# Attention, gated product and a second layer in one kernel: three weight conversions of the first batch moved behind its last group, two filling products fewer, and the second batch's groups four steps later

## The chip, the cores and the metric

The kernel runs on one core of a Trainium2 chip. The metric is the device time of one execution in microseconds; the median of several executions counts. A profiled execution gives a trace, whose engines are named PE (TensorE, matrix products), PEld (its weight loads), ACT (ScalarE), DVE (VectorE) and SP (SyncE, which here issues every DMA on one queue).

## The reference, cut to what matters

```python
# q, k, v: 4 batches, 8 heads, 576 positions, 64 wide
scores = (q @ k.T) / 8          # heads 0-3: the last 32 positions
                                # heads 4-7: 32 positions, every 4th
attn = softmax(where(mask, scores, -1e9))
x = (attn @ v)                  # 2304 tokens x 512
a = x @ w_a; b = x @ w_b        # 512 x 1536 each
y = (a * b) @ w_out             # 1536 x 512
h = y @ w_in                    # 512 x 2048
g = max(h, 0) + alpha * min(h, 0)
out = g @ w_out2                # 2048 x 512
```

The weights arrive as 64-bit floats and are turned into 32-bit floats on the chip.

## The kernel before, in words

**Tiles and steps.** The 2304 tokens are four token tiles of 512, 512, 512 and 768 (TILES). The program is written as a row of numbered steps. `step(products)` runs what was hung on that step before the products (`before`), the products, what was hung behind them (`after`), one round of the running jobs (`convey`), and last the loads in `behind`. Steps 0 to 16 are the first batch's attention. Step 17 begins token tile 0: for each of 12 blocks f of 128 columns of w_a and w_b there are three steps, twelve products into bank pa (x times w_a), twelve into pb (x times w_b), and then `flush`, twelve products of the block before with w_out into four banks accA. In every twelve there are four chunks c, each of three products: high by high, high by low, low by high part (lines L518, L519, L520), since each 32-bit number is held as the sum of two shorter ones.

**Attention.** A batch has 12 groups of three query blocks. Group i passes in the first batch through: scores on PE in step i (sp, L377); `largest` on DVE (L392), which is interleaved with `weights` of the group before (L413, L415, L417); `exps` on ACT, three of them (L406); transposition on PE in step i + 2 (tp, L429), its copy by ACT (`moved`, L434); the product with v in step i + 3 (ap, L442), and `placed`, a copy into the high part of x by ACT (L471) and the low part by DVE (L478, L476). Chunk c of x is complete with group 3c + 2, so chunk 3 only with group 11, placed in step 14. The second batch's groups go in pairs beside token tile 0: `visit_scores` (banks sa) at the steps in `slots`, `visit_turn` three steps later. Token tile 1 takes their result.

**Conversions.** Number n of the weight conversions is a job in `queue`: n = 0 and 1 are w_a and w_b of block 0, 2 and 3 those of block 1, 4 is w_out of block 0, and so on, three for a block. It begins with its load, `lead` steps ahead of step k. From step k on it issues two ACT operations (L189, which scales the high words; L192, the low words), a DVE operation that joins them (L195), an ACT copy to the high part (L224) and a DVE subtraction for the low part (L227). The tuple `apart` spreads them over further steps. The joined 32-bit block is also stored to DRAM two steps later (wad, wof; L202), and a buffer of five has to wait for that store. Loads are L207; the loads of a group are L341 (q, k) and L346 (v), those of v into five places, so that v of group i waits for the product of group i - 5.

**Filling products.** `heat(n)` multiplies a tile of zeros into bank pb, which nobody reads then (L611). ZEROS gives their number for steps 0 to 11; there are also five ahead of step 0. `begin` starts block 0's pa and pb with the chunks of x that exist, in steps 12 to 14.

**Order.** Up to the end of step 22 `in_source_order` keeps PE, ACT and DVE in the order in which the code issues. Behind that a scheduler at compile time places the instructions on each engine by its own estimate. Every engine then runs its row in order. SP's row also holds stores, which wait for DVE, so a load can stand behind a store.

Of the kernel before, what the change touches and what calls it, by code (L numbers as in the profile page):

```python
# [24 lines left out]
NC = DM // 128  # L25
# [7 lines left out]
NG = NST // GS  # L33
# [2 lines left out]
TILES = [(0, 512), (512, 512), (1024, 512), (1536, 768)]  # L36
N_PLAIN = 3
ONCE = 4, 12
ZEROS_FIRST, ZEROS = 5, (3, 0) + 10 * (1,)

HT = 384
NP = NT // (2 * HT)
# [22 lines left out]
def tile_kernel(ctx: ExitStack, tc: tile.TileContext, qk, v, mask, wab, wo1, w2, alpha, out):  # L65
# [38 lines left out]
    xh, xl = cut(rt, 0, 4, 512), cut(rt, 2048, 4, 512)  # L104
# [39 lines left out]
    n_start = NC * NG + 5  # L144
    n_tiles = len(TILES)
    start_of = [n_start + 3 * NFA * t + t for t in range(n_tiles)]
# [3 lines left out]
    before, after, now = {}, {}, [0]  # L150

    def at_step(table, k, fn):
        table.setdefault(k, []).append(fn)

    def step(products=None):
        k = now[0]
        for fn in before.pop(k, []):
            fn()
        if products:
            products()  # L160
        for fn in after.pop(k, []):
            fn()
        if k not in held:
            convey()
        while behind:
            behind.pop(0)()
        now[0] += 1


    queue, belt, behind = [], [], []  # L170

    def convey():

        for job in belt[::-1 if now[0] < start_of[1] else 1]:
            if next(job, "end") == "end":
                belt.remove(job)
        while queue and queue[0][0] <= now[0]:
            job = queue.pop(0)[1]
            next(job)
            belt.append(job)  # L180
# [102 lines left out]
    ws, wo = {}, {}  # L283
# [54 lines left out]
    def load_qk(n):  # L338
        if n < B * NC * NG:
            tqs[n] = t = (qk_ring if n >= NC * NG else qk_first).next()  # L340
            in_order(n, nc.sync.dma_start(out=t, in_=qk[n // (NC * NG), n % (NC * NG)]))  # L341

    def load_v(n):
        if n < B * NC * NG:
            tvs[n] = t = (v_ring if n >= NC * NG else v_first).next()[:KT].rearrange("p (s j d) -> p s j d", j=2, d=D)
            in_order(n, nc.sync.dma_start(out=t, in_=v[n // (NC * NG), n % (NC * NG)]))  # L346
# [175 lines left out]
    def contract(acc, wh, wl, xh, xl, n, cs=range(NC)):  # L522
        for c in cs:
            mm3(acc[:, :n], wh[:, c * 128:(c + 1) * 128], wl[:, c * 128:(c + 1) * 128],
                xh[:, c, :n], xl[:, c, :n], c == 0, c == NC - 1)
# [13 lines left out]
    def bank(tag):  # L539
        return ps.tile([128, 512], F32, tag=tag, name=tag)  # L540
# [26 lines left out]
    xn[1] = cut(ft, 2048, 4, 512)  # L567

    for i in range(4, NC * NG + 3):
        at_step(after, max(0, i - 4) if i < NC * NG else i - 1, lambda i=i: behind.append(lambda: load_qk(i)))  # L570
    for i in range(1, NC * NG + 3):
        at_step(after, i - 1 if i < 3 else i if i < NC * NG else i + 5, lambda i=i: behind.append(lambda: load_v(i)))
    at_step(after, 1, lambda: behind.append(lambda: nc.sync.dma_start(out=mk[:, 2:], in_=mask[:, 2:])))
    first = [Group(0, i) for i in range(NC * NG)]
    stages = [(after, "moved", 2), (after, "placed", 3), (before, "scores", 0), (before, "transposed", 2)]
# [12 lines left out]
    due += [(3 * f + 5, 3 * f - 2, "o", f, 0) for f in range(NFA)]  # L588
    n, k = 0, 0
    while due:  # L590
        k = (7, 9, 11)[n] if n < 3 else max(k + 1, 13)
        lead = 2 if n < 2 else min(n + 2, 6) if n < ONCE[1] else 2
        apart = (1, 0, 1, 1) if n < 2 else (1, 0, 0, 1) if n < 3 else (0, 0, 0, 1 if k < n_start else 0)
        job = min((x for x in due if n_start + x[1] <= k), default=None)
        if job:
            due.remove(job)
            places = raw_once if ONCE[0] <= n < ONCE[1] else raw_ring
            if job[2] == "a":
                job_w(k - lead, lead, places, apart, *job[3:])
            else:  # L600
                job_o(k - lead, lead, places, apart, job[3])
            n += 1
# [18 lines left out]

    begun = []

    def begin(j, *cs):

        if not begun:
            begun.extend((bank("pa"), bank("pb")))
        contract(begun[j], ws[0][:, 2 * j], ws[0][:, 2 * j + 1], xh, xl, 512, cs)

    begins = len(nc.cur_bb.bb.instructions)  # L630
    heat(ZEROS_FIRST)
    for k in range(n_start):
        if k < 12:
            step(lambda: heat(ZEROS[k]))
        elif k < 15:
            step(lambda: [begin(*x) for x in (((0, 0),), ((0, 1),), ((0, 2), (1, 0, 1, 2)))[k - 12]])
        else:
            step()
    at_step(after, start_of[1], lambda: tc.keep_in_program_order(nc.sync.dma_start(out=al, in_=alpha)))
# [85 lines left out]
        for f in range(NFA):  # L725
            reload_o(start_of[t] + 3 * f, t, f)
    for t in range(3):
        slots = [start_of[t] + (3 if t == 0 else 0) + int(j * (2.5, 2.64, 2.3)[t]) for j in range(NC * NG)]
        groups = [Group(t + 1, i) for i in range(NC * NG)]
        pairs = [groups[j:j + 2] for j in range(0, NC * NG, 2)]  # L730
        for j in range(len(pairs) + 1):
            k = slots[2 * j] if j < len(pairs) else slots[-1] + 2
            visit_scores(k, pairs[j] if j < len(pairs) else [], pairs[j - 1] if j else [])
            if j < len(pairs):
                visit_turn(k + 3, pairs[j])
# [4 lines left out]
    for n, job in enumerate(jobs[JOBS_A:JOBS_P]):  # L740
        at, lead = JOBS_AT[n]
# [62 lines left out]
    k = start_of[N_PLAIN - 1]  # L804
# [24 lines left out]
    for t, (t0, n) in enumerate(TILES[:N_PLAIN]):  # L829
        assert now[0] == start_of[t], (now[0], start_of[t])  # L830
        if t < 2:
            xn[t + 2] = xn_pair if t else cut(ft, 0, 4, 512)
        for f in range(NFA):
            final = f == NFA - 1
            if f == 0:
                accs = None
            wf = ws[f]
            early = (t, f) == (0, 1)
            started = (t, f) == (0, 0)
            cs = [NC - 1] if started else range(NC)  # L840
            pa = begun[0] if started else bank("acc2" if early else "pa")
            g = g_tile(n)
            box = []
            at_step(after, now[0] + 1, lambda g=g, pa=pa: nc.scalar.copy(g, pa[:, :n]))
            step(lambda: contract(pa, wf[:, 0], wf[:, 1], xh, xl, n, cs))
            pb = begun[1] if started else bank("acc3" if early else "pb")
            k = now[0]
            at_step(after, k + 1, lambda g=g, pb=pb: nc.vector.tensor_tensor(out=g, in0=g, in1=pb[:, :n], op=ALU.mult))
            at_step(after, k + 1 if final else k + 2, lambda g=g, box=box: split_g(box, g, n))
            step(lambda: contract(pb, wf[:, 2], wf[:, 3], xh, xl, n, cs))  # L850
            if final and t + 1 < N_PLAIN:
                for c in range(NC):
                    at_step(after, now[0], lambda c=c: split_x(xh, xl, xn[t + 1], c, TILES[t + 1][1]))
            if f == 1:
                accs = new_accs(f"A{t}")
                prev = (accs, *prev[1:])
            step(flush if f else None)
            prev = (accs, wo_of(t, f), box, n, f, NFA, x1d, t)
            if (t, f) == (0, 1):
                in_source_order(begins)  # L860
        step(flush)
# [106 lines left out]
    for f in range(NFA):  # L968
# [4 lines left out]
        ws = factors.pop(f)  # L973
# [280 lines left out]
```

## Time and profile before

| what | value |
|---|---|
| runs | 878.32, 876.09 and 878.98 us, median 878.32 us |
| the profiled execution | 876.4 us, of which 874.6 us are its span |
| busy share of the span | PE 98%, PEld 89%, DVE 72%, ACT 61% |
| instructions | 15640 |

The profiled execution is 1.9 us under the median of the runs shown. Busy shares are means over the whole span; what a change in one place is worth is read from that place.

### The profile page before, as it was taken

The numbers are of one execution on the slowest core, as the hardware profiler recorded it, in microseconds if no ns is written. First come the engines' busy times: TensorE is split into PE (matmuls) and PEld (weight loads), VectorE is DVE, ScalarE is ACT, GpSimd is POOL, SyncE is SP. The second block draws the span as 40 slices with busy tenths as digits, with TensorE's granted clock in tenths as the row PEclk, the third lists the DMA queues.
The fourth block names the chain that finished last, engine by engine and source line by source line (L and its number), as shares of the span: only waits on it lengthen the run. The fifth ranks groups of instructions, "written<-read, shape, count | busy, mean of one in ns | idle before, by whom it ended". The sixth has DMA issues, their size and how long they took to land.

```text
span 874.6 us, 15640 instructions
## 1 busy us (share of the span) xinstructions
PE 861.2 (98%) x5418; PEld 781.5 (89%) x5418; DVE 628.0 (72%) x1450; ACT 537.5 (61%) x1195; POOL 0.7 (0%) x6
## 2 busy tenths in 40 slices
PE   8898999999999999999999999999999999999998
PEld 5677888888888887889999999999999999999998
DVE  5768773646767678869797837898565896567954
ACT  7889873555666567655554637775565855565542
POOL 0000000000000000000000000000000000000000
PEclk9799999999999999999999999999999999999999
DMA  9969961589799888999565559878888887778875
GB/s 278 348 203 350 352 210 61 172 283 334 253 322 330 290 294 284 324 314 316 192 229 170 192 213 303 260 240 262 275 243 245 256 268 224 230 247 258 272 223 184
DMA packets 108125, 225.28 MB, mean 258 GB/s; under 512 B 12304, under 2 KB 27408, under 8 KB 108048
## 3 DMA queue, kind: packets, MB, share of 16 engines
q1 hardware_dynamic: 108048, 224.30, 78.6%
q8 instruction: 43, 0.70, 0.3%
q14 instruction: 34, 0.28, 0.1%
HBM read 169.72 MB, written 54.53 MB: 256 GB/s over the span
## 4 chain that ended last, share of the span: by engine, by line
PE 89%; DMA 6%; DVE 3%; ACT 1%; issue 1%; SPq 1%; ACTq 0%; DVEq 0%
PE acc L1163 20%; PE at L869 12%; PE pb L869 8%; PE pa L869 8%; PE accA L518 4%; PE accA L519 4%; PE accA L520 4%; PE pa L518 4%; PE pa L519 4%; PE pa L520 4%; PE pb L518 4%; PE pb L519 3%; PE pb L520 3%; DMA wsd<-rt 3%; PE tp L429 2%; PE sa L442 2%
## 5 line engine op out<-in xcount | busy, mean ns | idle before, releaser
L1163 PE MATMUL acc<-rt 128*128 128x384 f32 x1008 | 187.6, 334 | 0.0
L1163 PEld LDWEIGHTS acc<-rt 128*128 128x128 f32 x1008 | 175.8, 188 | 0.4 <-ACT ft L1146 0.4
L278 ACT CAST rt<-ft 128x512 fp32r<-128x512 f32 (+3 forms) x165 | 103.6, 636 | 89.1 <-DMA wsd<-rt 22.8
L281 DVE TENSOR_TENSOR rt<-ft,rt 128x512 fp32r<-128x512 f32 (+3 forms) x165 | 115.8, 708 | 58.8 <-ACT rt L278 57.7
L869 PE MATMUL at<-rt 128*128 128x384 f32 x414 | 84.3, 335 | 0.0
L885 ACT COPY ft<-at 128x384 f32<-128x384 f32 x105 | 49.9, 475 | 51.6 <-PE at L869 51.0
L869 PEld LDWEIGHTS at<-rt 128*128 128x128 f32 x414 | 72.7, 188 | 0.5 <-ACT ft L885 0.4
L518 PE MATMUL accA<-rt 128*128 128x512 f32 (+1 forms) x160 | 62.5, 392 | 2.3 <-ACT rt L278 2.3
L519 PE MATMUL accA<-rt 128*128 128x512 f32 (+1 forms) x160 | 61.9, 387 | 0.2 <-DVE rt L281 0.2
L520 PE MATMUL accA<-rt 128*128 128x512 f32 (+1 forms) x160 | 61.2, 384 | 0.0
L406 ACT ACTIVATE ft<-ft 128x96 f32<-128x96 f32 x144 | 52.2, 367 | 12.6 <-DVE ft L392 12.6
L195 DVE SCALAR_TENSOR_TENSOR ft<-ft 128x512 uint32<-128x512 uint32 x60 | 41.2, 687 | 22.8 <-ACT ft L192 16.9
L281 DVE TENSOR_TENSOR rt<-gx,rt 128x768 fp32r<-128x768 f32 x43 | 41.1, 957 | 22.3 <-ACT rt L278 22.0
L869 PE MATMUL pb<-rt 128*128 128x384 f32 x276 | 56.0, 337 | 0.1
L869 PE MATMUL pa<-rt 128*128 128x384 f32 x276 | 55.2, 334 | 0.0
L869 PEld LDWEIGHTS pb<-rt 128*128 128x128 f32 x276 | 48.1, 188 | 1.8 <-DVE gx L882 0.9
L192 ACT ACTIVATE ft<-ft 128x512 uint32<-128x512 uint32 x60 | 40.4, 673 | 14.2 <-DMA ft<-in_w 14.1
L278 ACT CAST rt<-gx 128x768 fp32r<-128x768 f32 x43 | 36.0, 836 | 21.1 <-PE acc L1163 16.9
L869 PEld LDWEIGHTS pa<-rt 128*128 128x128 f32 x276 | 48.5, 188 | 0.0
L869 PE MATMUL at<-rt,rx 128*128 128x384 f32 x216 | 44.0, 337 | 1.5 <-ACT ft L885 1.5
L189 ACT ACTIVATE ft<-ft 128x512 f32<-128x512 f32 x60 | 40.1, 670 | 6.6 <-DMA ft<-in_w 5.7
L869 PEld LDWEIGHTS at<-rt,rx 128*128 128x128 f32 x216 | 37.7, 188 | 2.7 <-ACT ft L885 2.5
(157 smaller groups left out, 1763.5 us busy)
## 6 DMA issues: line engine op xcount, KB each, us to landing
rt<-wsd SPq DMA_DIRECT2D x318, 256.0 KB, 3.2
wsd<-rt SPq DMA_DIRECT2D x112, 256.0 KB, 5.0
ft<-in_w SPq DMA_DIRECT2D x32, 512.0 KB, 5.6
ft<-in_qk SPq DMA_DIRECT2D x48, 208.0 KB, 5.4
ft<-in_wab SPq DMA_DIRECT2D x19, 512.0 KB, 5.5
rt<-wod SPq DMA_DIRECT2D x19, 512.0 KB, 5.1
rx<-wod SPq DMA_DIRECT2D x17, 512.0 KB, 4.7
ft<-in_v SPq DMA_DIRECT2D x48, 144.0 KB, 5.7
```

The costliest lines, as they stand in the source:

```text
L189: held(nc.scalar.activation(f, high.bitcast(F32), AF.Prelu, scale=2.0 ** -112, alpha=-2.0 ** 32))
L192: nc.scalar.activation(low, low, AF.Copy, scale=0.933 * 2.0 ** -29)
L195: nc.vector.scalar_tensor_tensor(out=fi, in0=fi, scalar=3, in1=low, op0=ALU.logical_shift_left, op1=ALU.bitwise_or)
L278: hi_eng.copy(hi, x)
L281: lo_eng.tensor_tensor(out=lo, in0=x, in1=hi.bitcast(F32), op=ALU.subtract)
L406: nc.scalar.activation(self.et[:, s], self.st[:, s], AF.Exp, bias=self.sm[:, 0, s:s + 1], scale=-1.0, accum_out=self.sm[:, 1, s:s + 1])
L518: nc.tensor.matmul(acc, lhsT=wh, rhs=rh, start=first, stop=False)
L519: nc.tensor.matmul(acc, lhsT=wh, rhs=rl, start=False, stop=False)
L520: nc.tensor.matmul(acc, lhsT=wl, rhs=rh, start=False, stop=last)
L869: nc.tensor.matmul(acc[:, :HT], lhsT=a, rhs=x[:, b, c], start=start and c == k == 0, stop=c == 1 and k == 2, skip_group_check=not start,)
L885: nc.scalar.copy(out, acc[:, :HT])
L1163: nc.tensor.matmul(acc[a][:, :HT], lhsT=u, rhs=q[:, b, i % 2], start=new and first and k == 0, stop=last and k == 2, skip_group_check=not new,
```

## The change: what it does

Conversions 1, 2 and 3 begin at steps 10, 15 and 16 (they began at 9, 11 and 13), and the ACT copy of conversion 1 now stands behind the last group's `placed`. Conversions from 4 on go at step 18 and after, one in each step (14 and after). Their loads move with them. The filling products of steps 5 and 6 go (one each). Block 0's pb is not begun early: all its twelve products stand in step 18, and pa's chunks 0 and 1 are in step 12, chunk 2 in step 14. The second batch's first visit goes from step 20 to step 24 and the visits follow each other a little more closely; the last goes from step 49 to step 50. Its first three loads of q and k move four steps later, those of v one.

```diff
-ZEROS_FIRST, ZEROS = 5, (3, 0) + 10 * (1,)
+ZEROS_FIRST, ZEROS = 5, (3, 0, 1, 1, 1, 0, 0, 1, 1, 1, 1, 1)
+HEAD = (7, (1, 0, 1, 1)), (10, (1, 0, 2, 0)), (15, (0, 0, 0, 0)), (16, (1, 0, 0, 0))
...
-        at_step(after, max(0, i - 4) if i < NC * NG else i - 1, lambda i=i: behind.append(lambda: load_qk(i)))
+        at_step(after, max(0, i - 4) if i < NC * NG else i + 3, lambda i=i: behind.append(lambda: load_qk(i)))
...
-        k = (7, 9, 11)[n] if n < 3 else max(k + 1, 13)
-        lead = 2 if n < 2 else min(n + 2, 6) if n < ONCE[1] else 2
-        apart = (1, 0, 1, 1) if n < 2 else (1, 0, 0, 1) if n < 3 else (0, 0, 0, 1 if k < n_start else 0)
+        k, apart = HEAD[n] if n < 4 else (max(k + 1, 18), (0, 0, 0, 1 if k < n_start + 4 else 0))
+        lead = (2, 3, 4, 4)[n] if n < 4 else 5 if n < ONCE[1] else 2
...
-            step(lambda: [begin(*x) for x in (((0, 0),), ((0, 1),), ((0, 2), (1, 0, 1, 2)))[k - 12]])
+            step(lambda: [begin(c) for c in ((0, 1), (), (2,))[k - 12]])
...
-        slots = [start_of[t] + (3 if t == 0 else 0) + int(j * (2.5, 2.64, 2.3)[t]) for j in range(NC * NG)]
+        slots = [start_of[t] + (7 if t == 0 else 0) + int(j * (2.25, 2.64, 2.3)[t]) for j in range(NC * NG)]
...
-            pb = begun[1] if started else bank("acc3" if early else "pb")
+            pb = bank("acc3" if early else "pb")
...
-            step(lambda: contract(pb, wf[:, 2], wf[:, 3], xh, xl, n, cs))
+            step(lambda: contract(pb, wf[:, 2], wf[:, 3], xh, xl, n))
```

The lines of the changed kernel are one higher than those named above, up to some 640.

ACT's row from the exps of group 11 on, before; L189 and L192 are first operations of conversions, L224 their copies, tp and ap with a number the groups:

```order
L406 ACTIVATE ft<-ft 128x96 x3
L189 ACTIVATE ft<-ft 128x512
L434 COPY ft<-tp_10_474 96x384
L471 CAST rt<-ap_9_478 128x128
L471 CAST rt<-ap_9_478 128x48
L192 ACTIVATE ft<-ft 128x512
L224 CAST rt<-ft 128x512
L434 COPY ft<-tp_11_503 96x384
L471 CAST rt<-ap_10_507 128x80
L471 CAST rt<-ap_10_507 128x96
L189 ACTIVATE ft<-ft 128x512
L192 ACTIVATE ft<-ft 128x512
```

and the same place now:

```order
L407 ACTIVATE ft<-ft 128x96 x3
L193 ACTIVATE ft<-ft 128x512
L435 COPY ft<-tp_10_464 96x384
L472 CAST rt<-ap_9_468 128x128
L472 CAST rt<-ap_9_468 128x48
L435 COPY ft<-tp_11_493 96x384
L472 CAST rt<-ap_10_497 128x80
L472 CAST rt<-ap_10_497 128x96
L472 CAST rt<-ap_11_512 128x32
L472 CAST rt<-ap_11_512 128x128
L225 CAST rt<-ft 128x512
L190 ACTIVATE ft<-ft 128x512
```

Of the conversions only the second operation of conversion 1 is left between the exps of group 11 and its `placed`; the copy of conversion 1 and the whole of conversions 2 and 3 stand behind it.

SP's row from the load of v for group 6 (in_v) to that of group 9 and one row on, before; in_wab and in_wo are loads of weights:

```order
L346 DMA ft<-in_v 96x384
L207 DMA ft<-in_wab 128x512 x2
L341 DMA ft<-in_qk 128x416
L346 DMA ft<-in_v 96x384
L207 DMA ft<-in_wab 128x512
L207 DMA rf<-in_wab 128x512
L346 DMA ft<-in_v 96x384
L207 DMA rf<-in_wo 128x512
L346 DMA ft<-in_v 96x384
L207 DMA rf<-in_wab 128x512
```

and now, from the same load of v on:

```order
L347 DMA ft<-in_v 96x384
L208 DMA ft<-in_wab 128x512
L342 DMA ft<-in_qk 128x416
L347 DMA ft<-in_v 96x384 x4
L208 DMA ft<-in_wab 128x512
L347 DMA ft<-in_v 96x384
L208 DMA ft<-in_wab 128x512
L203 DMA wad<-ft 128x512
L208 DMA rf<-in_wo 128x512
L208 DMA rf<-in_wab 128x512 x2
```

From there to the load of v for group 9 there were five weight loads and now there is one; the store of conversion 0 now stands ahead of the weight loads from number 4 on.

PE's row where block 2's pb and the first flush stand, before; accA_0 to accA_3 are the flush's banks, pa here is already block 3's:

```order
L518 MATMUL pa<-rt 128x512
L518 MATMUL pb<-rt 128x512
L519 MATMUL pb<-rt 128x512
L520 MATMUL pb<-rt 128x512
L518 MATMUL pb<-rt 128x512
L519 MATMUL pb<-rt 128x512
L520 MATMUL pb<-rt 128x512
L518 MATMUL pb<-rt 128x512
L519 MATMUL pb<-rt 128x512
L518 MATMUL accA_0_671<-rt 128x512
```

and the place of the first flush now, straight behind block 1's pb (acc_600):

```order
L521 MATMUL acc_600<-rt 128x512
L519 MATMUL accA_0_619<-rt 128x512
L520 MATMUL accA_0_619<-rt 128x512
L378 MATMUL sa_0_665<-ft 64x96 x2
L378 MATMUL sa_1_666<-ft 64x96 x2
L378 MATMUL sa_0_665<-ft 64x96 x2
L378 MATMUL sa_1_666<-ft 64x96 x2
L521 MATMUL accA_0_619<-rt 128x512
L519 MATMUL accA_1_620<-rt 128x512
```

Before, the scheduler had put the first product of block 3's pa ahead of block 2's pb and the first flush into the middle of that pb; now the flush of block 0 begins ahead of block 2. From token tile 1 on PE's row is the same in both kernels.

## Rows read from the trace of the kernel before

**Rows 1.** The page, its first line.

```profile
span 874.6 us, 15640 instructions
```

**Rows 2.** Waits of PE over the span: us in total, times, longest.

```profile
PE at L869 <- ACT ft L885: 1.5, 2, 0.8
```

**Rows 3.** Windows: length; busy PE, PEld, DVE, ACT, POOL (instructions); granted clock; DMA share; GB/s.

```profile
5.00:10.00 5.00, 3.85 (x57) 2.61 (x55) 2.73 (x25) 3.85 (x20) 0.00 (x0) 1.00 1.04 294
...
25.00:30.00 5.00, 2.69 (x34) 1.88 (x32) 3.53 (x19) 4.73 (x20) 0.00 (x0) 0.82 1.03 327
30.00:35.00 5.00, 5.00 (x29) 3.31 (x29) 2.72 (x12) 3.63 (x11) 0.00 (x0) 0.50 1.05 359
35.00:40.00 5.00, 5.00 (x25) 4.00 (x23) 4.34 (x11) 4.53 (x10) 0.00 (x0) 0.66 1.04 398
...
65.00:70.00 5.00, 2.69 (x12) 1.93 (x11) 4.66 (x23) 5.00 (x18) 0.00 (x0) 1.00 1.00 335
```

**Rows 4.** Timeline of PE: start, us, instruction, [idle before <- releaser].

```profile
15.92 0.39 PE L611 MATMUL pb<-zeros 128*128 128x512 bf16 x1
16.24 0.71 PE L377 MATMUL sp<-ft 64*64 64x96 f32 x12
...
27.16 0.57 PE L442 MATMUL ap<-ft 96*64 96x64 f32 x12 [1.43 <-ACT rt L224]
...
29.14 0.91 PE L442 MATMUL ap<-ft 96*64 96x64 f32 x12 [0.69 <-DMA ft<-in_v]
...
41.14 0.73 PE L377 MATMUL sa<-ft 64*64 64x96 f32 x24
...
44.66 0.39 PE L518 MATMUL acc<-rt 128*128 128x512 f32 x1
...
47.38 0.39 PE L518 MATMUL pa<-rt 128*128 128x512 f32 x1
```

**Rows 5.** Chain of work that ended last, first 45 us: start, us, what.

```profile
19.75 9.26 DMA ft<-in_v
```

**Rows 6.** Timeline of ACT, first batch.

```profile
17.45 0.47 ACT L434 COPY ft<-tp 96x384 f32<-96x384 f32 x1
...
18.17 0.38 ACT L406 ACTIVATE ft<-ft 128x96 f32<-128x96 f32 x1
...
19.26 0.66 ACT L189 ACTIVATE ft<-ft 128x512 f32<-128x512 f32 x1
...
25.94 0.69 ACT L192 ACTIVATE ft<-ft 128x512 uint32<-128x512 uint32 x1
26.48 0.65 ACT L224 CAST rt<-ft 128x512 fp32r<-128x512 f32 x1
...
27.77 0.49 ACT L471 CAST rt<-ap 128x32 fp32r<-128x32 f32 x2 [0.27 <-PE ap L442]
28.02 0.37 ACT L406 ACTIVATE ft<-ft 128x96 f32<-128x96 f32 x1
...
35.58 0.48 ACT L471 CAST rt<-ap 128x32 fp32r<-128x32 f32 x2
```

**Rows 7.** Timeline of DVE, weights of group 11.

```profile
30.06 0.16 DVE L413 TENSOR_SCALAR ft<-ft 128x3 f32<-128x3 f32 x1
...
30.47 0.46 DVE L417 TENSOR_TENSOR ft<-ft 128x288 f32<-128x288 f32 x1
```

**Rows 8.** Timeline of DVE, low part of conversion 11.

```profile
63.27 0.69 DVE L227 TENSOR_TENSOR rt<-ft,rt 128x512 fp32r<-128x512 f32 x1 [1.16 <-ACT rt L224]
```

**Rows 9.** Timeline of PE, blocks 2 and 3.

```profile
50.93 0.50 PE L518 MATMUL pa<-rt 128*128 128x512 f32 x1 [0.68 <-ACT ft L844]
...
69.72 0.97 PE L518 MATMUL accA<-rt 128*128 128x512 f32 x3 [2.31 <-ACT rt L278]
```

**Rows 10.** DMA from 65 to 110 us: packets, bytes, rate.

```profile
DMA packets 6453, 15.65 MB, mean 348 GB/s; under 512 B 736, under 2 KB 2080, under 8 KB 6450
```

**Rows 11.** DMA from 43 to 65 us.

```profile
DMA packets 1820, 4.31 MB, mean 196 GB/s; under 512 B 205, under 2 KB 496, under 8 KB 1816
```

More of the change, by code (lines that the diff above doesn't have):

```diff
@@ L569, in tile_kernel @@
     for i in range(4, NC * NG + 3):
-        at_step(after, max(0, i - 4) if i < NC * NG else i - 1, lambda i=i: behind.append(lambda: load_qk(i)))
+        at_step(after, max(0, i - 4) if i < NC * NG else i + 3, lambda i=i: behind.append(lambda: load_qk(i)))
     for i in range(1, NC * NG + 3):
-        at_step(after, i - 1 if i < 3 else i if i < NC * NG else i + 5, lambda i=i: behind.append(lambda: load_v(i)))
+        at_step(after, i - 1 if i < 3 else i if i < NC * NG else i + 6, lambda i=i: behind.append(lambda: load_v(i)))
     at_step(after, 1, lambda: behind.append(lambda: nc.sync.dma_start(out=mk[:, 2:], in_=mask[:, 2:])))
@@ L622, in tile_kernel, with begin @@
     begun = []
-    def begin(j, *cs):
+    def begin(c):
         if not begun:
-            begun.extend((bank("pa"), bank("pb")))
-        contract(begun[j], ws[0][:, 2 * j], ws[0][:, 2 * j + 1], xh, xl, 512, cs)
+            begun.append(bank("pa"))
+        contract(begun[0], ws[0][:, 0], ws[0][:, 1], xh, xl, 512, [c])
     begins = len(nc.cur_bb.bb.instructions)
```

## The prediction

> **What bounds the kernel now.** I read the waits of PE first. What it waits for lies almost wholly in the first 75 us: after that only one pair of waits of 1.5 us in all is over half a microsecond [rows 2]. So a microsecond that PE gains early is kept to the end, and the question is only what the first 75 us lose. I then read windows of 5 us. From 25 to 30 us PE is busy 2.69 of 5 us, and from 28 us on the clock granted to TensorE is halved (1.2 instead of 2.4 GHz): shares 0.82, 0.50 and 0.66 in three windows [rows 3]. At full speed these would have held 5 x (0.18 + 0.50 + 0.34) = 5.1 us more of PE's time. Then I read PE's timeline for what came before the fall: a wait of 1.43 us at 27.16 and one of 0.69 us at 29.14, both ahead of a product with v [rows 4]. The chain of waits names the cause: the load of v for group 9, issued at 19.75 us, took 9.26 us to land [rows 5], with DMA's share at 1.03 in that stretch [rows 3]; five weight loads stand between the loads of v for groups 6 and 9 on SP. The wait at 27.16 is put down to ACT: with an ACT copy for a conversion, 26.48, just ahead of it, the in-order row of ACT is the other half of the trouble [rows 6]. Last, PE's later timeline has two more waits, 0.68 us at 50.93 and 2.31 us at 69.72 [rows 9].
>
> **The change, part by part.**
> *First batch, ACT.* From the exps of group 7 (18.17) to those of group 11 (28.02) ACT runs nearly without a gap [rows 6]. In that piece two conversions' ACT operations stand; now one of them, the second operation of conversion 1, goes behind the exps of group 11: 26.48 - 25.94 = 0.54 us. The 0.27 us wait at 27.77 was for a product delayed by the loads and goes too [rows 6]. A filling product costs PE 16.24 - 15.92 = 0.32 us [rows 4]; two go, but ACT was nearly full beside them, so they bring between 0 and 0.64 us. I take 0.3. Exps of group 11 then start at 28.02 - 0.54 - 0.27 - 0.3 = 26.9.
> *From there to block 1.* With durations as an upper estimate: exps 1.09 (19.26 - 18.17) to 28.0; second operation of conversion 1 0.54 to 28.5; copy of group 10 0.47 to 29.0; `placed` of group 9 0.49 to 29.5 [rows 6]. DVE's weights of group 11 take 30.47 + 0.46 - 30.06 = 0.87 [rows 7], to 28.9, and the transposition fits in by 29.5. Copy of group 11 0.47 to 30.0; its product with v 0.57 at the full clock [rows 4] to 30.5; `placed` 0.49 to 31.0; copy of conversion 1 0.65 to 31.7 [rows 6]; DVE's low part 0.69 [rows 8] to 32.4. Block 0's pb, all twelve products, takes 47.38 - 44.66 = 2.72 us [rows 4]; two of the first three need no low part, so it ends at about 35.0. Block 1 can begin there. Before, the second batch's scores at 41.14 stood in that place and are now later: 41.1 - 35.0 = **6.1 us**. Not beginning pb early costs what PE idles around 31 us, which is in this sum. This supposes that TensorE's clock stays up. The two ends: if it is low for as long as before, the 5.1 us above go and 1.0 us is left; if ACT's operations overlap as their starts in the rows do, about 1 us more, 7.1 us.
> *Loads of v.* Group 9's v is now behind one weight load instead of five. Its place comes free with group 4's product, near 17 us; even at 9.26 us again it would land at 26.5, when that product is due.
> *Conversions 2 and 3.* Six ACT operations behind `placed` of group 11. Conversion 2 needs 0.66 + 0.69 + 0.65 on ACT [rows 6] and two DVE operations of 0.69 [rows 8]: ready near 35, when block 1's pa starts and its first two products need only the high part. Conversion 3 has until block 1's pb, 2.72 us later. No cost taken; up to 1 us if the chain is later than worked out.
> *Block 3's early product and the flush of block 2.* The wait of 0.68 us is that of a product of block 3's pa for the copy of block 2's pa, which stood right ahead of it in PE's row; a flush stands between them now. The wait of 2.31 us is that of block 2's flush for a split which ACT reached late, with the second batch's exps ahead of it; those come four steps later, and ACT's row at that time is emptier by them. Both go: 0.68 + 2.31 = **3.0 us** [rows 9].
> *Conversions from 4 on, four steps later.* The work is the same. From a conversion's end to the step that needs it there were seven steps and are three, some 9.5 us. DMA has to move 0.79 MB for a conversion (128 x 1024 words of four bytes in, half as many out) and in the mean 0.16 MB for the visits (two groups' 352 KB in 4.5 steps) in each step; a step is 2.72 us and a share of a visit, about 3.2 us, so 297 GB/s are wanted where 348 were moved from 65 to 110 us [rows 10]. It is hidden if the three steps hold. The store of conversion 0 that now stands ahead of weight loads waits for DVE until about 23 us, when nothing behind it is due before 33.
> *New waits* that the fixed rows of ACT and SP may bring cannot be read off: between 0 and the 2.31 us of the worst one shown [rows 9]; I take 0.5, as the work per step is under what each engine can do.
> *Sum*, against the profiled execution: 876.4 - 6.1 - 3.0 + 0.5 = 867.8 (its span is 874.6 us [rows 1], and 1.8 us around it stay). That execution lies 1.9 us below the median of the runs shown (878.32), so the median forecast is **869.7**.
>
> A rule speaks against it. The row first: in the window from 5 to 10 us PE is busy only 3.85 of 5 us and the clock stays at 1.00, but from 25 to 30 us with 2.69 of 5 it falls [rows 3]. The Trainium skill, page "TensorE: Matmul & The Clock Gate", section "A second HAM failure mode: psum-queue depth-cycling", says that many short idle spells of PE between groups of products can make the clock drop again and again. Steps 5 and 6, without a filling product and paced by ACT, are such spells; by that rule the clock would fall there already, by the row it does not. What that would cost stands under the first rival.
>
> **The rivals.**
> *The clock falls again in the first batch*, in the two steps without filling products or in the spells near 26 and 31 us. For it: the waits of 1.43 and 0.69 us were enough before [rows 4]. Against it: now I find under 1 us of idle in such a stretch instead of these 2.1, and from 65 to 70 us PE is busy as little as from 25 to 30 with the clock at 1.00 [rows 3]. If it is low for as long as before, the 5.1 us come back: 867.8 + 5.1 + 1.9 = 874.8.
> *The gain is partly given back at the weights.* Block 4's pa now comes, by 35.0 + 9 x 2.72 (three pairs, three flushes) + 2.7 for the visits, at 62.2, while the low part of conversion 11, which it needs, ended at 63.27 + 0.69 = 64.0 before [rows 8]. Were it no earlier, PE would wait 1.8 us: 871.5. Against it: ACT idles less and has fewer exps ahead.
> *Slower: the three steps do not hold.* From 43 to 65 us DMA moved only 196 GB/s [rows 11], since SP stood at stores. 4.31 MB in 22 us are 4.5 steps' need where PE passes 7; one such stretch makes the weights 2.5 steps late, which three steps of reserve cover. It decides from a reserve overrun by 2.7 steps (8.6 us), so from a bit over two such stretches. With three, 7.5 - 3 = 4.5 steps x 3.2 = 14.4 us: 867.8 + 14.4 + 1.9 = 884. Against it: from 65 us on DMA kept 348.
> *Nothing moves*: the loads of v are late anyway and the chain of ACT sets the same end: 878. Against it stands the one load instead of five.
>
> **How the numbers follow.** Chances: forecast 0.60 (its own range 867.5 to 871.2, from 7.1 instead of 6.1 us to 2.3 us of new waits, less rounding), clock 0.15, weights given back 0.15, slower 0.07, nothing 0.03. The predicted time is 869.7. The range reaches to the clock's case, which leaves out the last two and the very best: 866.5 to 875.2. About 0.3% (2.6 us) is what a measurement of this kernel can tell from no change; by the cases, faster 0.90, within it 0.03, slower 0.07.
>
> **What would show it.** Right: granted clock 1.00 in all windows from 20 to 45 us; exps of group 11 near 27; block 1's pa (bank acc2) near 35; no wait of PE over 1 us between 35 and 75; the second batch's first scores only after the start of block 0's flush. Wrong: a share under 1.00 near 17 or 28 us; PE waiting in token tile 0 for low parts of conversions (L228 or L225 as releaser); loads of v again 9 us under way.

## The result and the profile after

| | before | after |
|---|---|---|
| median of 4 runs | 878.15 us (876.09 to 878.98) | 867.32 us (866.77 to 868.62) |
| profiled execution | 876.4 us, span 874.6 us | 867.85 us, span 866.1 us |

The ratio is 0.9882, with a 95% interval of 0.9861 to 0.9903: 10.8 us less. Between the two profiled executions it is 8.55 us.

I read the windows of 5 us first (length; busy PE, PEld, DVE, ACT, POOL with their instructions; granted clock; DMA share; GB/s):

```profile
20.00:25.00 5.00, 4.40 (x68) 3.19 (x68) 4.05 (x25) 5.00 (x25) 0.00 (x0) 1.00 0.75 230
25.00:30.00 5.00, 4.00 (x39) 2.85 (x40) 4.05 (x24) 4.57 (x19) 0.00 (x0) 1.00 0.96 348
30.00:35.00 5.00, 4.86 (x41) 3.58 (x40) 3.57 (x13) 4.38 (x11) 0.00 (x0) 1.00 0.89 297
35.00:40.00 5.00, 5.00 (x24) 4.14 (x23) 2.99 (x5) 4.17 (x9) 0.00 (x0) 1.00 0.98 322
```

PE is busy 4.00 us from 25 to 30 us, where it was 2.69, and the granted clock stays at 1.00 where it was 0.82, 0.50 and 0.66 [rows 3]. ACT's timeline has the exps of group 11 at 27.08 us and one conversion operation (28.15) between them and the three `placed` copies of groups 9, 10 and 11:

```profile
27.08 0.39 ACT L407 ACTIVATE ft<-ft 128x96 f32<-128x96 f32 x1
...
28.15 0.69 ACT L193 ACTIVATE ft<-ft 128x512 uint32<-128x512 uint32 x1
...
29.06 0.51 ACT L472 CAST rt<-ap 128x128 fp32r<-128x128 f32 x2
30.23 0.48 ACT L435 COPY ft<-tp 96x384 f32<-96x384 f32 x1 [0.66 <-PE tp L430]
30.74 0.48 ACT L472 CAST rt<-ap 128x80 fp32r<-128x80 f32 x2
31.37 0.48 ACT L472 CAST rt<-ap 128x32 fp32r<-128x32 f32 x2
```

The last of them is at 31.37 where it was at 35.58 [rows 6]. PE's timeline:

```profile
29.70 0.49 PE L430 MATMUL tp<-ident,ft 128*96 128x128 f32 x3
...
35.84 0.39 PE L519 MATMUL acc<-rt 128*128 128x512 f32 x1
...
41.28 0.39 PE L519 MATMUL accA<-rt 128*128 128x512 f32 x1
...
41.83 0.56 PE L378 MATMUL sa<-ft 64*64 64x96 f32 x16
```

Block 0 is done and block 1's pa begins at 35.84 us; the second batch's scores stood in that place at 41.14 [rows 4]. I call this place the end of block 0 below: it is 5.3 us earlier, one execution against one. The waits of PE over the whole span (total, times, longest), without that of the start:

```profile
PE tp L430 <- ACT ft L407: 1.4, 2, 0.8
...
PE tp L430 <- DVE ft L418: 1.0, 3, 0.6
PE sp L378 <- PE ap L443: 0.8, 3, 0.3
PE at L869 <- ACT ft L885: 0.6, 1, 0.6
```

No wait for a load of v is left in the first batch; the waits of 0.68 and 2.31 us in token tile 0 [rows 9] are gone; the one at L869, 1.5 us before [rows 2], is 0.6. The profiled gain is accounted for: 5.3 + 0.68 + 2.31 = 8.3 of 8.55 us, and in token tile 1, where PE's rows are the same, it stands 8.3 us earlier (156.33 against 164.64). Waits behind 180 us sum to 1.4 us, where they summed to 1.95.

### The profile page after: what moved, and what is told of

Its sections match the earlier page's. It is cut to its first block, busy times and chain, and to the rows that moved or that the text cites. A ratio compares the mean times of both kernels' runs of the same rounds, so it can differ in the third digit from the quotient of the medians.

```text
span 866.1 us, 15636 instructions
## 1 busy us (share of the span) xinstructions
PE 856.2 (99%) x5412; PEld 779.0 (90%) x5416; DVE 627.5 (72%) x1450; ACT 536.5 (62%) x1195; POOL 0.7 (0%) x6
## 4 chain that ended last, share of the span: by engine, by line
PE 76%; DMA 12%; DVE 6%; ACT 4%; issue 1%; SPq 0%; ACTq 0%; DVEq 0%
PE acc L1163 20%; PE at L869 12%; PE pb L869 8%; PE pa L869 8%; DMA wsd<-rt 5%; DMA ft<-in_w 4%; PE accA L519 3%; PE accA L521 3%; PE accA L520 3%; PE pa L519 2%; PE pb L519 2%; PE pa L521 2%; PE pa L520 2%; PE pb L521 2%; PE pb L520 2%; DVE rt L282 1%
## 5 line engine op out<-in xcount | busy, mean ns | idle before, releaser
L869 PE MATMUL at<-rt 128*128 128x384 f32 x414 | 84.3, 335 | 0.0
L869 PEld LDWEIGHTS at<-rt 128*128 128x128 f32 x414 | 72.7, 188 | 0.4 <-ACT ft L885 0.2
L869 PE MATMUL pb<-rt 128*128 128x384 f32 x276 | 55.9, 337 | 0.3 <-DVE gx L882 0.3
L869 PE MATMUL pa<-rt 128*128 128x384 f32 x276 | 55.3, 334 | 0.0
L869 PEld LDWEIGHTS pb<-rt 128*128 128x128 f32 x276 | 48.1, 188 | 1.6 <-DVE gx L882 1.1
L869 PEld LDWEIGHTS pa<-rt 128*128 128x128 f32 x276 | 48.5, 188 | 0.0
L869 PE MATMUL at<-rt,rx 128*128 128x384 f32 x216 | 43.9, 336 | 0.6 <-ACT ft L885 0.6
L869 PEld LDWEIGHTS at<-rt,rx 128*128 128x128 f32 x216 | 37.8, 188 | 1.8 <-ACT ft L885 1.7
```

What stands on the lines that cost most here:

```text
L869: nc.tensor.matmul(acc[:, :HT], lhsT=a, rhs=x[:, b, c], start=start and c == k == 0, stop=c == 1 and k == 2, skip_group_check=not start,)
```

## The experiments

The theory after the result: the first batch lost its time to two things, loads of v queued behind weight loads and ACT's row with two conversions in it; the fall of the clock comes with them; and the two later waits go with the conversions. Rivals: the fillers, the second batch's later place or the clock alone bring the gain. A ratio is always to the kernel before on the same chip.

**1 and 2. Each half of the change alone.** `e1_conversions_only` is the changed kernel with the fillers and the second batch's loads and visits of before:

```diff
-ZEROS_FIRST, ZEROS = 5, (3, 0, 1, 1, 1, 0, 0, 1, 1, 1, 1, 1)
+ZEROS_FIRST, ZEROS = 5, (3, 0) + 10 * (1,)
...
-        at_step(after, max(0, i - 4) if i < NC * NG else i + 3, lambda i=i: behind.append(lambda: load_qk(i)))
+        at_step(after, max(0, i - 4) if i < NC * NG else i - 1, lambda i=i: behind.append(lambda: load_qk(i)))
...
-        at_step(after, i - 1 if i < 3 else i if i < NC * NG else i + 6, lambda i=i: behind.append(lambda: load_v(i)))
+        at_step(after, i - 1 if i < 3 else i if i < NC * NG else i + 5, lambda i=i: behind.append(lambda: load_v(i)))
...
-        slots = [start_of[t] + (7 if t == 0 else 0) + int(j * (2.25, 2.64, 2.3)[t]) for j in range(NC * NG)]
+        slots = [start_of[t] + (3 if t == 0 else 0) + int(j * (2.5, 2.64, 2.3)[t]) for j in range(NC * NG)]
```

> The changed kernel with the second batch's visits and loads where they were before and with all the old filling products. Theory A (first batch and token tile 0 are two separate gains): the first batch's 5.3 us stay and the two later waits of PE, 0.68 and 2.31 us, come back, 872 to 874 us. Theory B (the later waits went because the scheduler put the flushes elsewhere, which follows from the conversions): they stay away, 868 to 870 us.

`e2_visits_only` is the kernel before with the last three of these edits the other way round:

```diff
-        slots = [start_of[t] + (3 if t == 0 else 0) + int(j * (2.5, 2.64, 2.3)[t]) for j in range(NC * NG)]
+        slots = [start_of[t] + (7 if t == 0 else 0) + int(j * (2.25, 2.64, 2.3)[t]) for j in range(NC * NG)]
...
```

> The kernel before with only the second batch's visits and loads moved. Theory A: only the later waits go, 3.0 us, about 875 us, and the clock still falls near 28 us. Theory B: PE's row of the flushes stays as before and so do the waits, 877 to 879 us.

Measured: e1 869.46 us, ratio 0.9922 [0.9896, 0.9948]; e2 875.37 us, 0.9970 [0.9950, 0.9991]. In e1 block 0 ends at 36.47 us at a clock of 1.00, and neither of the two later waits is left:

```profile
36.47 0.73 PE L378 MATMUL sa<-ft 64*64 64x96 f32 x24
```

In e2 these are the waits of PE from 40 to 80 us:

```profile
PE tp L429 <- DVE ft L413: 1.4, 1, 1.4
PE pa L518 <- ACT ft L844: 0.7, 1, 0.7
```

The 2.31 us wait for a split on ACT (L278) is gone from here as well, though conversions are where they were, and the 0.68 us one (L844) is still there. So the conversions bring some 7 to 8 us (by the ratio and by the medians) and take both waits away; the visits bring some 2 to 3 and take the longer one away by themselves, in its place a wait of 1.4. That exchange is worth only 0.9 us. The rest of the gain in e2's profiled execution lies in the first batch, in two windows and at block 1's first product:

```profile
25.00:30.00 5.00, 2.53 (x31) 2.00 (x33) 3.94 (x21) 5.00 (x22) 0.00 (x0) 0.93 1.04 293
30.00:35.00 5.00, 5.00 (x37) 3.49 (x37) 2.71 (x10) 3.62 (x10) 0.00 (x0) 0.73 1.04 357
...
38.35 0.39 PE L518 MATMUL acc<-rt 128*128 128x512 f32 x1
```

ACT's row and the loads of v behind weight loads are there as in the kernel before, and PE still waits 1.1 us for v, but the slow clock takes 5 x (0.07 + 0.27) = 1.7 us instead of 5.1, and block 0 ends 2.8 us earlier than at 41.14. The loads of q and k that move in e2 change little there: the load of v for group 11 lands at 33.4 instead of 33.7 us. So the 41.14 us of the kernel before looks like one execution of a place that can differ by up to 3 us, and the distances from it below (e4, e7, e9, e11, e12) have that uncertainty; the medians decide.

**3 and 4. The order of the loads of v.** `e3_v_first`, the kernel before with the loads of v for groups 5 to 11 two steps earlier, put the loads of groups 3, 4 and 5 out of order in their places, so it computes with some blocks of v exchanged:

```diff
-        at_step(after, i - 1 if i < 3 else i if i < NC * NG else i + 5, lambda i=i: behind.append(lambda: load_v(i)))
+        at_step(after, i - 1 if i < 3 else i - 2 if 5 <= i < NC * NG else i if i < NC * NG else i + 5, lambda i=i: behind.append(lambda: load_v(i)))
```

> The kernel before, with the loads of v for groups 5 to 11 issued two steps earlier in the code, so that that of group 9 has fewer weight loads ahead; conversions untouched. If the late load of v makes PE idle and so the clock fall, this gives 3 to 5 us by itself: 873 to 875 us, granted clock 1.00 to 45 us. If ACT's backlog of conversions is what holds the chain: at most 1 us, 877 to 878 us, and the clock falls as before.

880.59 us, 1.0032 [1.0012, 1.0051]; PE stood 5.1 us at one load of v. That tells nothing of the question; experiment 9 asks it properly. `e4_early_loads` leaves ACT's row as in the changed kernel and puts weight loads ahead of loads of v again:

```diff
-        lead = (2, 3, 4, 4)[n] if n < 4 else 5 if n < ONCE[1] else 2
+        lead = (2, 3, 8, 8)[n] if n < 4 else 10 if n < ONCE[1] else 2
...
-            in_order(n, nc.sync.dma_start(out=t, in_=v[n // (NC * NG), n % (NC * NG)]))
+            in_order(n + (NC * NG if n > 6 else 0), nc.sync.dma_start(out=t, in_=v[n // (NC * NG), n % (NC * NG)]))
```

> The changed kernel with the weight loads back in the old places on SP, ahead of the loads of v for groups 7 to 11; ACT's row as changed. If the late load of v is the cause: the load takes 8 to 9 us again, PE waits for it, the clock falls, 871 to 873 us. If ACT's row is the cause: 867 to 868 us.

872.84 us, 0.9944 [0.9925, 0.9963], 5.5 us over the changed kernel. A piece of the chain of its first 48 us (start, us, what):

```profile
20.91 8.98 DMA ft<-in_v
```

PE's timeline between 22 and 33 us, the rows with a wait for v, and block 1's first product:

```profile
24.06 0.57 PE L443 MATMUL ap<-ft 96*64 96x64 f32 x12 [1.43 <-DMA ft<-in_v]
...
27.81 0.57 PE L443 MATMUL ap<-ft 96*64 96x64 f32 x12 [1.75 <-DMA ft<-in_v]
...
30.02 0.91 PE L443 MATMUL ap<-ft 96*64 96x64 f32 x12 [1.00 <-DMA ft<-in_v]
...
40.42 0.39 PE L519 MATMUL acc<-rt 128*128 128x512 f32 x1
```

And its window from 30 to 35 us:

```profile
30.00:35.00 5.00, 4.97 (x33) 3.81 (x34) 2.10 (x8) 1.71 (x5) 0.00 (x0) 0.50 1.02 339
```

The 9 us load of [rows 5] is back, 4.2 us of waits with it, the clock at 0.50, and block 0 ends at 40.42 us. ACT is busy 1.71 of 5 us there, so it isn't ACT. The order of the loads, with the fall of the clock that follows, is worth 4.6 us in the first batch, even with ACT's row mended. From 40 to 80 us PE has no wait, so the two later waits don't hang on the loads.

**5 and 6. The fillers.** `e5_old_fillers` is the changed kernel with the two fillers back, `e6_no_fillers` the changed kernel with none in steps 2 to 11:

```diff
-ZEROS_FIRST, ZEROS = 5, (3, 0, 1, 1, 1, 0, 0, 1, 1, 1, 1, 1)
+ZEROS_FIRST, ZEROS = 5, (3, 0) + 10 * (1,)
```

```diff
-ZEROS_FIRST, ZEROS = 5, (3, 0, 1, 1, 1, 0, 0, 1, 1, 1, 1, 1)
+ZEROS_FIRST, ZEROS = 5, (3, 0) + 10 * (0,)
```

> The changed kernel with the filling products of steps 5 and 6 back. As predicted they are worth 0.3 us (0 to 0.64): 867.3 to 868.0 us, and the exps of group 11 start 0.3 us later. If they keep the clock up: no difference, since it is at 1.00 without them.

> The changed kernel with no filling product in steps 2 to 11 (those ahead of step 0 and in step 0 stay). If the filling products hold the clock, as the rival of the prediction has it: a granted clock under 1.00 between 10 and 35 us and 870 to 873 us. If PE's own work of the groups holds it: 1.00 everywhere and, as ACT sets the pace, 866.3 to 867.3 us.

e5: 868.68 us, 0.9895 [0.9859, 0.9931], end of block 0 at 35.47: the two fillers taken out make no difference that can be measured. e6: 870.54 us, 0.9909 [0.9877, 0.9940]; two of its windows:

```profile
20.00:25.00 5.00, 3.82 (x66) 2.81 (x64) 4.04 (x27) 5.00 (x25) 0.00 (x0) 1.00 0.82 268
25.00:30.00 5.00, 4.15 (x35) 3.00 (x36) 3.99 (x23) 4.66 (x19) 0.00 (x0) 0.77 0.92 293
```

and PE's timeline:

```profile
25.30 0.50 PE L430 MATMUL tp<-ident,ft 128*96 128x128 f32 x3 [0.93 <-ACT ft L407]
...
26.85 0.50 PE L430 MATMUL tp<-ident,ft 128*96 128x128 f32 x3 [0.55 <-DVE ft L418]
...
36.98 0.39 PE L519 MATMUL acc<-rt 128*128 128x512 f32 x1
```

Without any filler the clock falls to 0.77 behind waits of 0.53 (at 22.73 us), 0.93 and 0.55 us, where the changed kernel has 0.25, 0.61 and 0.55 and stays at 1.00, and block 0 ends 1.1 us later. The intervals of e6 and of the changed kernel overlap, so that this costs time is likely, not shown.

**7. The clock alone.** `e7_dense_fill` is the kernel before with four fillers instead of one in steps 10 and 11.

```diff
-ZEROS_FIRST, ZEROS = 5, (3, 0) + 10 * (1,)
+ZEROS_FIRST, ZEROS = 5, (3, 0) + 8 * (1,) + (4, 4)
```

> The kernel before with four filling products instead of one in steps 10 and 11, which lie in PE's idle time ahead of the late products with v. If the fall of the clock, and not the late load itself, is the larger part of the loss (5.1 us of PE time by the windows): the clock stays at 1.00 and the time is 873 to 875 us. If the chain of loads and ACT sets the end of the first batch at either clock: 877 to 878.5 us.

877.13 us, 0.9999 [0.9978, 1.0019]. The granted clock is 1.00 in every window from 10 to 65 us, but block 0 ends at 39.86, only 1.3 us earlier. PE's timeline says why:

```profile
27.88 0.57 PE L442 MATMUL ap<-ft 96*64 96x64 f32 x12 [1.46 <-ACT rt L224]
...
35.05 0.57 PE L442 MATMUL ap<-ft 96*64 96x64 f32 x12 [1.35 <-DMA ft<-in_v]
...
39.86 0.73 PE L377 MATMUL sa<-ft 64*64 64x96 f32 x24
...
68.44 1.48 PE L518 MATMUL accA<-rt 128*128 128x512 f32 x3 [2.32 <-ACT rt L278]
```

with a piece of the chain:

```profile
27.47 7.44 DMA ft<-in_v
```

The load of v for group 11 lands at 34.9 us, and PE, faster now, stands before it. In the kernel before the same load was issued at 26.59 us, took 7.1 and so landed near 33.7, and its product began at 34.63 without a wait. So the loads set the end in e7; how much of the 5.1 us they would hide in the kernel before is not shown, since here this load is also 1.2 us later. The last row of the timeline gives a second reading: the 2.3 us wait is still there, and in this execution the clock falls at it:

```profile
65.00:70.00 5.00, 2.68 (x10) 1.70 (x10) 4.66 (x21) 5.00 (x19) 0.00 (x0) 0.87 0.90 316
70.00:75.00 5.00, 5.00 (x22) 4.03 (x21) 3.93 (x7) 5.00 (x12) 0.00 (x0) 0.79 0.98 337
```

Behind the wait the second batch's next scores start at 77.24 us (76.92 in the kernel before), so the 1.3 us are lost there with 0.3 more; the two shares are 5 x (0.13 + 0.21) = 1.7 us of full speed. In the profiled execution of before the same wait left the clock at 1.00 [rows 3].

**8. Where the last 0.8 us of the first batch lie.** `e8_begin_spread` gives block 0's chunks of pa a step each, so that group 11's transposition has three products fewer ahead of it.

```diff
-step(lambda: [begin(c) for c in ((0, 1), (), (2,))[k - 12]])
+step(lambda: [begin(c) for c in ((0,), (1,), (2,))[k - 12]])
```

> The changed kernel with chunk 1 of block 0's pa in step 13 instead of step 12, so that PE turns group 11 three products earlier (ACT waits 0.66 us for it in the changed kernel). If that wait is on the path: block 1 begins 0.5 us earlier, 866.6 to 867.0 us. If PE's products only change places: 867.3 us.

869.41 us, 0.9900 [0.9868, 0.9931]. The transposition starts 0.5 us earlier, at 29.18, but block 0 ends at 36.37, with 0.5 us of the second batch's scores now inside it (at 32.62). Without them it would end where it did: the products only change places, and the 0.8 us are not that wait.

**9 and 10. Loads of v earlier, in order.** `e9_v_in_order` is the kernel before with those loads two steps earlier for all groups from 3 on, `e10_after_v_early` the changed kernel with them one step earlier.

```diff
-        at_step(after, i - 1 if i < 3 else i if i < NC * NG else i + 5, lambda i=i: behind.append(lambda: load_v(i)))
+        at_step(after, i - 1 if i < 3 else i - 2 if i < NC * NG else i + 5, lambda i=i: behind.append(lambda: load_v(i)))
```

```diff
-        at_step(after, i - 1 if i < 3 else i if i < NC * NG else i + 6, lambda i=i: behind.append(lambda: load_v(i)))
+        at_step(after, i - 1 if i < 3 else i - 1 if i < NC * NG else i + 6, lambda i=i: behind.append(lambda: load_v(i)))
```

> The kernel before, with the loads of v for groups 3 to 11 issued two steps (some 5 us) earlier in their old order; conversions, their ACT operations and the second batch's visits stay. Theory A (the late loads of v alone set the end of the first batch): no wait of PE over 0.5 us for a load of v between 20 and 35 us, and block 1's pa, whose place behind the second batch's first scores was at 44.1 us in the kernel before (41.14 for the scores), starts some 4 us earlier, scores at 37 us; time 873 to 874 us, ratio near 0.995. Theory B (ACT's row with two conversions in it sets the end as well): waits for v go, waits for ACT's placed copies and weights copies take their place, the scores stay at 39 to 41 us and the time is 876 us or more. Rival C: DMA is full there, so the loads of v only push the weight loads late, which gives the same time with waits for conversions in token tile 0.

(The 44.1 us in it is a slip; the place is 41.14.)

> The changed kernel, with the loads of v for groups 3 to 11 one step earlier in their order. If loads of v still cost PE something there, block 1's pa starts before 35.5 us (35.84 in the changed kernel) and the time is 866 to 867 us; if ACT's row alone sets the end of the first batch now, it starts at 35.8 and the time is the changed kernel's, 867.3 us, within 1 us.

e9: 876.63 us, 1.0012 [0.9987, 1.0036]. e10: 868.55 us, 0.9900 [0.9868, 0.9932], end of block 0 at 35.61: the loads cost the changed kernel nothing more. PE's timeline of e9:

```profile
27.36 0.50 PE L429 MATMUL tp<-ident,ft 128*96 128x128 f32 x3 [0.94 <-ACT rt L224]
...
30.00 0.50 PE L520 MATMUL pa<-rt 128*128 128x512 f32 x1 [0.98 <-DVE rt L227]
...
38.98 0.73 PE L377 MATMUL sa<-ft 64*64 64x96 f32 x24
```

No wait for v is left. The wait at 27.36 is put down to a copy on ACT (L224), but the transposition needs the weights of group 10, which DVE ended at 27.2, behind the exps that ACT, busy all 5 us from 25 to 30, had reached late:

```profile
26.76 0.45 DVE L417 TENSOR_TENSOR ft<-ft 128x288 f32<-128x288 f32 x1
```

The wait at 30.00 is for the low part of conversion 0 on DVE (L227), which stands there behind low parts of `placed` that waited 0.9 us for ACT, and behind an operation of conversion 1. Block 0 ends 2.2 us earlier, with the clock at 0.72 from 30 to 35 us, and the median doesn't move. From 40 to 80 us PE waits as before, 0.7 and 2.3 us, so rival C (conversions late in token tile 0) doesn't show. Theory A is refuted; B's time and waits came, and the place, 38.98, just under its 39: ACT's row is a limit of its own.

**11 and 12. Loads and clock together, conversions as before.** `e11_v_and_clock` is e9 with the fillers of e7; `e12_again` is the same kernel, profiled once more.

```diff
-ZEROS_FIRST, ZEROS = 5, (3, 0) + 10 * (1,)
+ZEROS_FIRST, ZEROS = 5, (3, 0) + 8 * (1,) + (4, 4)
...
-        at_step(after, i - 1 if i < 3 else i if i < NC * NG else i + 5, lambda i=i: behind.append(lambda: load_v(i)))
+        at_step(after, i - 1 if i < 3 else i - 2 if i < NC * NG else i + 5, lambda i=i: behind.append(lambda: load_v(i)))
```

> The kernel before with both the earlier loads of v and four filling products instead of one in steps 10 and 11, so that neither a load of v nor the clock should hold back the first batch, while two conversions stay in ACT's row and the visits stay. Theory A' (before the change three limits of nearly the same height stood on each other, loads of v, clock and ACT's row; ACT's is what is left here): granted clock 1.00 from 15 to 45 us, no wait for v, the second batch's first scores at 37.5 to 38.5 us (41.14 in the kernel before, 38.98 with the earlier loads alone), ratio 0.994 to 0.999. Rival (ACT's row is no limit of its own): scores at 36.5 us or earlier and a ratio under 0.993. Rival (DMA as a whole is full and gives the time back later): scores early, ratio 1.00.

> The kernel before with earlier loads of v and four filling products in steps 10 and 11, once more, for a second profile: the first showed the second batch's scores at 37.22 us (41.14 before) at a granted clock of 1.00, and the median over ten executions was no shorter all the same. If the early gain is in every execution and given back later, the scores stand at 37 to 38 us again and PE's waits behind 180 us sum to 4 us or more (4.3 in the first profile, 2.0 in the kernel before). If the first profile was a lucky execution, the scores stand at 39 us or later with a clock under 1.00 between 20 and 40 us.

e11: 877.51 us, 0.9996 [0.9976, 1.0016]; e12: one execution, 874.88 us. The window from 30 to 35 us in e11:

```profile
30.00:35.00 5.00, 4.63 (x40) 3.39 (x40) 3.37 (x14) 4.56 (x12) 0.00 (x0) 1.00 1.04 397
```

PE's timeline there, at the end of block 0:

```profile
29.66 0.50 PE L520 MATMUL pa<-rt 128*128 128x512 f32 x1 [0.98 <-DVE rt L227]
...
37.22 0.72 PE L377 MATMUL sa<-ft 64*64 64x96 f32 x24
```

The same window in e12:

```profile
30.00:35.00 5.00, 4.53 (x33) 3.05 (x34) 3.26 (x14) 4.55 (x14) 0.00 (x0) 0.70 1.04 396
```

and the same places in e12's timeline:

```profile
30.09 0.50 PE L520 MATMUL pa<-rt 128*128 128x512 f32 x1 [0.98 <-DVE rt L227]
...
39.08 0.72 PE L377 MATMUL sa<-ft 64*64 64x96 f32 x24
```

One kernel, two executions: with the clock at 1.00 block 0 ends at 37.22, with 0.70 and (from 35 to 40 us) 0.95 it ends 1.9 us later. Of these 0.4 were there ahead of the fall (30.09 against 29.66), so the slow clock cost 1.4 us where its shares make 5 x (0.30 + 0.05) = 1.75 us of full speed: once loads don't cover it, most of the clock's price is on the path. At 1.00 and with no load late, 1.4 us are left to the changed kernel's 35.84; the wait of 0.98 us for the low part of conversion 0 lies in them, so most of it is ACT's row and what hangs on it.

That the 2 to 4 us gained here do not show in the median is in part explained. By what was expected of it, e12 makes e11's first profile a lucky execution: its place is 39.08, at a clock under 1.00. And e11 shows the signs of its last rival, early scores and a ratio of 1.00: of its 3.9 us, 0.7 go in token tile 0, where PE's waits sum to 3.7 instead of 3.0 us, and 2.35 behind 180 us, where they sum to 4.3 instead of 1.95 (3.0 in e12). That leaves 0.85, and the span is 0.8 us shorter. Only 0.96 us of those waits are for a DMA, so that a full DMA gives the time back is not shown. Nor is it the clock: at a mean granted clock of 0.998 five executions of e11 average 877.1 us, and five of the kernel before on that chip 876.3. Why the ten executions come out no faster stays open; only two executions of this kernel were profiled.

No run takes apart what else came with the conversions: in every run of the changed kernel block 0's pb is not begun early, and what that does by itself is not shown.

## Why the prediction was right, step by step

*First batch, ACT.* Exps of group 11: 26.9 predicted, 27.08 measured. From there the sum was 0.8 us too small: block 1's pa came at 35.84, not 35.0. The step that was off is "the transposition fits in by 29.5": it stood behind six products of pa in PE's row and began at 29.70, ACT waited 0.66 us for it, and the last `placed` began at 31.37 instead of 30.5. So 5.3 us in place of the term of 6.1, against the one execution that ends at 41.14. The 0.3 us for two fillers cannot be told from nothing (e5).

*Loads of v.* Right, and larger than the text made it: their order is worth 4.6 us in the first batch by itself (e4). The prediction also gave them too little. It put the wait of 1.43 us at 27.16 down to ACT, as the profile does, and called ACT's row the other half of the trouble there. SP's row and its landing time say otherwise, for the load of v for group 8:

```profile
18.04 0.33 SPq L346 DMA_DIRECT2D ft<-in_v  x1
...
ft<-in_v SPq DMA_DIRECT2D x1, 144.0 KB, 9.0
```

It landed at 27.0, and the product at 27.16 is the one that needs it; no operand of that product comes from the copy L224. In e7 the same wait, also put down to L224, ends when that load lands (18.90 + 8.8 = 27.7). In e9, where it is issued earlier and ACT's row is as before, the product starts at 25.85 without a wait. So both waits ahead of the fall of the clock were for loads of v, and ACT's row is the limit that stands behind them. The order of the loads is not enough by itself (e9), and ACT's row is not either: e4 kept 0.7 us of the 5.3 in its profiled execution, and by the medians 4.7 us, of which the two later waits are 3.0. The two limits and the clock stood at nearly the same height, so that taking away one leaves most of the time to the next.

*The clock.* "If it is low for as long as before, the 5.1 us above go" took the whole fall as lying on the path. The runs show less and not one figure: 1.3 us came back in e7, where a load set the end; in e2, where 3.4 us less were lost to the clock, block 0 ended 2.8 us earlier; without late loads it was 1.4 us for 1.75 (e11 and e12). With the fillers in place the changed kernel's execution shows 1.00 throughout, with waits of 0.61, 0.55 and 0.19 us from 25 to 30 us, more than the "under 1 us" that the prediction counted on; without them (e6) the clock falls in the window from 25 us, where PE is busy 4.15 us, and not in the one from 20 us with 3.82. The rule of the Trainium skill that the prediction weighed (page "TensorE: Matmul & The Clock Gate", section "A second HAM failure mode: psum-queue depth-cycling") expects falls at repeated short idle spells. The trace of e6 shows one such fall, after 25 us, and none at the shorter waits ahead of it; that of the changed kernel shows none.

*The later waits.* 3.0 us predicted, 3.0 us gone. For the 2.31 us the reason given, the second batch's exps, is enough (e2), but the place of the conversions is so too (e1). The 0.68 us go with the conversions and not with the visits (e1, e2).

*New waits.* 0.5 us taken; for low parts of conversions there are one of 0.19 at 28.67, in the first batch, and one of 0.16 at 42.55, in token tile 0. The rival at the weights didn't come: block 4's pa starts at 64.29 us without a wait. The slower rival didn't either; from 43 to 65 us DMA now moves 337 GB/s where it was 196 [rows 11]:

```profile
DMA packets 3239, 7.41 MB, mean 337 GB/s; under 512 B 375, under 2 KB 1103, under 8 KB 3235
```

*From the profile to the median.* The sum was 867.8 and the profiled execution is 867.85. That they agree so closely is luck: the first batch gave 0.8 us less than its term, the new waits took some 0.3 less than theirs, and the waits behind 180 us, which the sum left as they were, are 0.6 us shorter. The mis-sized term is the 1.9 us added for the median: the changed kernel's median lies 0.5 us under its profiled execution. So the measured 867.32 lies 0.2 us under the forecast's own range (867.5 to 871.2; the terms named for its lower end, 1.0 and 0.5 us, lead only to 868.2) and inside the stated one. An offset of before's own executions was carried over as if it belonged to any kernel. They scatter with the clock: in the 28 of the first set the five of the lowest mean granted clock (0.992) average 879.4 us and the five of the highest (0.998) 875.8; the changed kernel's four show 0.999 to 1.00. Most of the gain isn't the clock, then: in the set of e9 and e10 the five executions of the kernel before at 0.998 average 874.5 us, and the four of e10, at 0.999 to 1.00, 868.6. What makes them scatter, the wait near 28 us and perhaps the one near 69 at which the clock fell in e7, is what the change removed. That is argued from e2, e7, e11 and e12; of the kernel before only one execution was profiled.

## What to carry to other kernels

Where PE stands still, list every engine and queue that comes due within a microsecond of it: here loads, ACT's row and the clock each hid the other two, and each mended alone gave 0 to 5 us of the 11 (the 5, in e4, with the two later waits in it). When a wait is put down to an engine whose result the instruction doesn't use, work out when its loads landed. Put work that nobody needs yet (here conversions and their loads) behind the last urgent operation on every in-order row it crosses, SP's too. When a median is forecast from one execution, ask whether the change removes what makes executions differ before its offset is added.

## What the runs showed that I had not expected

A wait of the same length at the same place left the clock at 1.00 in one kernel and brought it to 0.87 and 0.79 in another (2.31 us in before, 2.32 us in e7), with 1.6 us lost around it. More waiting need not bring a longer fall: from 25 to 30 us PE was busy 2.69 us in before and 2.53 in e2, and the slow clock took 5.1 us of full speed in the one and 1.7 in the other. The loads of v for groups 7 to 11, 144 KB each, took 7.1 to 9.3 us in the kernel before and 8.1 to 9.0 in e4, with weight loads between them on the queue, and 2.6 to 6.5 in the changed kernel.
